# A planned order for attention and a gated MLP on one core: each DMA counted with its pieces and a limit of eight, other gates for kept weights, and new offsets

## The chip, the core and the metric

The kernel runs on one core of one Trainium2 chip. The metric is the device time of one execution in microseconds (us). A core has five engines with an instruction queue each: TensorE (PE) for matmuls, VectorE (DVE), ScalarE (ACT), GpSimd (POOL), and SyncE (SP), which here does nothing but issue DMAs. Every engine works its queue in order: an instruction that waits holds up all that stands behind it on that engine.

## The reference

```python
# q, k, v: (8, 8, 576, 64) float32; g_norm: (64,)
# moe_w_in: (512, 2048) float64, moe_w_out: (2048, 512) float64
kv  = np.einsum('bhsd,bhse->bhde', k, v)
out = np.einsum('bhsd,bhde->bhse', q, kv)
rms = np.sqrt(np.mean(out * out, axis=-1, keepdims=True) + 1e-06)
attn = (out / rms * g_norm).astype(np.float32)
x = attn.transpose(0, 2, 1, 3).reshape(4608, 512)
h = x @ w_in                       # 4608 x 2048
g = h * np.cos(h)
result = (g @ w_out).astype(np.float32)   # 4608 x 512
```

Nearly all of the arithmetic is in the two products with w_in and w_out.

## The kernel before, in words

**Tiling.** The 4608 tokens are cut into nine chunks of 512, the 2048 columns of w_in into sixteen pieces of 128, j = 0 to 15. Each operand of a product is split into a high and a low float32r part, and a product is three matmuls (high by high, high by low, low by high). The weights come as float64; their bits are taken apart and joined to float32 on ACT and DVE (`w_part`), then split.

**Stages.** Attention gives the x tiles of a chunk, four per chunk (p = 0 to 3, two heads each): `x_front_part` for chunks 0 and 1, `x_part` for the others. An x tile of the later kind begins with a load of q in four DMAs for each batch that the chunk touches (`q_loads`: eight where it touches two), then a transpose on DVE (`qT`). Chunks 0 to 2 are worked by 48 *steps* (chunk, j): `stage1_part` makes h for 128 columns in a PSUM bank, `act_part` makes g = h cos h on ACT and DVE (ki, r, then the split into ghi and glo), and `stage2_part` multiplies it into the accumulators acc. The order of the steps is chunk 0 with j 0 to 3, chunk 1 with j 0 to 7, then the remainders of both, then chunk 2; partial results of the first two segments go to DRAM and come back later (`part`). One step is 24 matmuls of 512 columns.

**Pairs.** Chunks 3 to 8 are worked two at a time. There the first product is done with seven products in place of eight (`quad_part`): the four quarters A11 to A22 of the operands and sums and differences of them, S1 to S4. `cross_part` makes these of the x tiles, `sums_part` makes them of w_in, once, piece pair m = 0 to 7 at a time. The split weights don't stay in SBUF: during the steps they are stored in DRAM, w_in's quarters and w_out by `keep_in` and `keep_out`, w_in's sums by `sums_part`; the arrays are `wq` and `wod`. From the first pair on they are loaded back as they are needed (`load_in`, `load_out`), and the space of the weights holds the operands of the pairs. The x tiles of chunks 3 and 4 are stored in DRAM too when they are ready (`x<-slot` in the profile) and come back when there is room for them (`wo<-x`, `xhi<-x`, `xlo<-x`).

**The order.** All of this is written as generators that yield requests: run on an engine for a modelled time with a priority (an earlier due time goes first), wait for events, take a buffer. `Order.run` is a small planner that runs while the kernel is built: it takes the request that can start first, by its own model of when engines are busy, and in that order the instructions are emitted and pinned. So the modelled costs decide the place of every instruction on its engine, and nothing of the model is in the kernel itself. On the chip an instruction starts as soon as its operands are there and its engine has come to it, so a DMA can be issued long before or after its planned time. The model has half speed for PE in the beginning and behind gaps (`slow`), and one access path that POOL and DVE share for some operations (`POOL*`, `DVE*`). The table `haste` holds an offset in us to the due time for each piece of work, found by a search outside the kernel; `put_off` reads it, and `step_off` reads offsets of gates, a quarter of the value in whole steps. A gate is an event that fires when the first product of a step, or a product of a pair, is planned, and lets other work begin.

**DMA in the model before.** `load` and the other senders request "SP" for the issue time of all their DMAs together (`issue_us`), emit them, then request "DMA" for a data time (`us`), one after the other, and the data count as landed `DMA_LAT` = 1.9 us later. In the trace SP at times waits for an earlier DMA to land before it issues the next one; the model before has no such limit.

All instructions go through a helper class, so that the profile puts nearly every one at line 225; groups are told apart by the names of their tiles.

Of the kernel before, what the change touches and what calls it, by code (L numbers as in the profile page):

```python
# [49 lines left out]
class Order:  # L50
# [84 lines left out]
    def run(self):  # L135
        while self.pending:
# [18 lines left out]
            proc = item[4]  # L155
# [16 lines left out]
def tile_kernel(  # L172
# [129 lines left out]
    KEEP, SUMS = 16, 18  # L302
# [3 lines left out]
    def due(i):  # L306
# [7 lines left out]
        ('acc', 0): -5.4, ('acc', 1): 203.3, ('acc', 10): 61.1, ('acc', 11): -32.4, ('acc', 12): -0.2,  # L314
        ('acc', 13): 113.7, ('acc', 14): 49.1, ('acc', 15): 149.6, ('acc', 16): -14.2, ('acc', 17): -14.6,
        ('acc', 19): -52.9, ('acc', 2): 50.3, ('acc', 20): 60.1, ('acc', 21): 215.4, ('acc', 22): -12.9,
        ('acc', 23): 75.5, ('acc', 24): 241.3, ('acc', 25): -23.3, ('acc', 26): -47.0, ('acc', 27): -6.6,
        ('acc', 29): 28.5, ('acc', 30): -51.1, ('acc', 31): 111.0, ('acc', 32): 20.4, ('acc', 33): 133.8,
        ('acc', 34): -195.5, ('acc', 35): 47.6, ('acc', 36): 59.4, ('acc', 37): 7.2, ('acc', 38): -35.1,
        ('acc', 39): -9.7, ('acc', 4): 124.9, ('acc', 40): -86.2, ('acc', 41): 247.6, ('acc', 42): 70.7,  # L320
        ('acc', 43): 6.6, ('acc', 44): 11.9, ('acc', 46): -38.4, ('acc', 47): 9.9, ('acc', 5): -14.3,
        ('acc', 6): 49.4, ('acc', 7): -37.8, ('acc', 8): 18.3, ('acc', 9): -0.2, ('act', 0): -46.6,
        ('act', 1): -60.5, ('act', 10): 39.5, ('act', 11): 33.6, ('act', 12): -13.8, ('act', 13): -156.4,
        ('act', 14): 13.0, ('act', 15): -102.7, ('act', 16): 17.7, ('act', 17): 24.0, ('act', 18): -19.1,
        ('act', 19): -12.1, ('act', 2): -180.3, ('act', 20): 9.6, ('act', 21): 49.5, ('act', 22): 2.2,
        ('act', 23): -118.6, ('act', 24): 5.8, ('act', 25): 59.1, ('act', 26): -1.5, ('act', 27): 229.0,
        ('act', 28): -66.9, ('act', 29): -40.3, ('act', 3): -10.9, ('act', 30): -95.6, ('act', 31): -40.1,
        ('act', 32): 2.5, ('act', 33): 2.9, ('act', 34): -17.2, ('act', 36): -21.4, ('act', 37): -50.0,
        ('act', 38): -51.6, ('act', 4): -0.4, ('act', 40): 14.6, ('act', 41): -7.3, ('act', 42): 28.4,
        ('act', 43): 112.9, ('act', 44): 0.7, ('act', 45): 176.9, ('act', 46): -31.5, ('act', 47): -36.8,  # L330
        ('act', 6): 2.1, ('act', 7): -3.0, ('act', 8): 20.7, ('act', 9): 22.9, ('combine by', 0, 0, 1): -15.7,
# [1352 lines left out]
```

## Time and profile before

| what | value |
|---|---|
| median of 3 runs (lowest, highest) | 848.12 us (846.54, 849.31) |
| profiled execution: its own time | 848.17 us |
| its span, first to last instruction | 846.4 us |
| PE busy, share of the span | 826.7 us, 98% |
| DVE, ACT, POOL busy | 602.0, 501.3, 236.0 us |
| mean granted clock of PE | 0.989 |
| DMA bytes, mean rate | 181.22 MB, 214 GB/s |

The span is what the views of the profile cover; the execution's own time holds 1.8 us more. Busy time is the time in which an engine had at least one instruction under way. Idle time of PE and a granted clock below 1 are what PE loses; an idle stretch of another engine counts only where PE ends up waiting for it. The DMA rows tell issues and the median time from issue to landing; a row of SPq in the order of time is SP's time at the issue itself, with any wait inside it.

### The profile page before, as it was taken

The numbers are of one execution on the slowest core, as the hardware profiler recorded it, in microseconds if no ns is written. First come the engines' busy times: TensorE is split into PE (matmuls) and PEld (weight loads), VectorE is DVE, ScalarE is ACT, GpSimd is POOL, SyncE is SP. The second block draws the span as 40 slices with busy tenths as digits, with TensorE's granted clock in tenths as the row PEclk, the third lists the DMA queues.
The fourth block names the chain that finished last, engine by engine and source line by source line (L and its number), as shares of the span: only waits on it lengthen the run. The fifth ranks groups of instructions, "written<-read, shape, count | busy, mean of one in ns | idle before, by whom it ended". The sixth has DMA issues, their size and how long they took to land.

```text
span 846.4 us, 12697 instructions
## 1 busy us (share of the span) xinstructions
PE 826.7 (98%) x4376; PEld 683.9 (81%) x4376; DVE 602.0 (71%) x953; ACT 501.3 (59%) x984; POOL 236.0 (28%) x151
## 2 busy tenths in 40 slices
PE   6999999999989998999999999999999999999998
PEld 6778888888877886888888888888888888888886
DVE  4898899748767888888899789788686621466111
ACT  3888786436445465686777657767566523465321
POOL 2410000223225463213332771452242011101211
PEclk7999999999999999999999999999999999999999
DMA  9997006896485597888678657876557657663663
GB/s 308 321 367 250 12 0 236 268 300 185 148 265 172 136 279 218 263 256 267 218 214 305 209 195 191 245 226 203 193 174 250 190 188 244 193 196 108 230 207 135
DMA packets 150913, 181.22 MB, mean 214 GB/s; under 512 B 74432, under 2 KB 114112, under 8 KB 150848
## 3 DMA queue, kind: packets, MB, share of 16 engines
q1 hardware_dynamic: 150336, 179.68, 67.7%
q8 instruction: 35, 0.57, 0.3%
q10 hardware_dynamic: 512, 0.72, 0.2%
q14 instruction: 30, 0.25, 0.1%
HBM read 143.66 MB, written 36.70 MB: 213 GB/s over the span
## 4 chain that ended last, share of the span: by engine, by line
PE 59%; DMA 3%; DVE 1%; ACT 1%; SPq 1%; POOL 0%; issue 0%; DVEq 0%
PE acc L225 31%; PE bank L225 28%; DMA sg<-in_v_dram 1%; SPq L225 1%; DMA x<-slot 1%; ACT wi L225 0%; POOL rinv L225 0%; DVE slot L225 0%; DMA qb<-in_q_dram 0%; DMA wo<-x 0%; DVE xlo L225 0%; DVE sg L225 0%; DVE wi L225 0%; ACT ghi L225 0%; DVE r L225 0%
## 5 line engine op out<-in xcount | busy, mean ns | idle before, releaser
L225 PE MATMUL acc<-wo,ghi 128*128 128x512 f32 x1152 | 356.4, 390 | 0.0
L225 PEld LDWEIGHTS acc<-wo,ghi 128*128 128x128 f32 x1152 | 214.9, 188 | 44.1
L225 PE MATMUL bank<-wi,wo 128*128 128x512 f32 (+2 forms) x1092 | 245.0, 379 | 4.5 <-ACT wi L225 2.9
L225 PEld LDWEIGHTS bank<-wi,wo 128*128 128x128 f32 (+2 forms) x1092 | 192.2, 185 | 46.5 <-ACT wi L225 4.1
L225 PE MATMUL acc<-wo,glo 128*128 128x512 f32 x576 | 224.3, 389 | 0.0
L225 POOL TENSOR_TENSOR rinv<-ms,mhalf 128x16 f32<-128x16 f32 (+1 forms) x36 | 99.2, 2759 | 149.4 <-DVE ms L225 143.4
L225 PEld LDWEIGHTS acc<-wo,glo 128*128 128x128 f32 x576 | 108.1, 188 | 22.7
L225 PE MATMUL bank<-xhi,wi 128*128 128x512 f32 x320 | 100.7, 396 | 3.3 <-DVE r L225 3.3
L225 POOL TENSOR_TENSOR glo<-wo,ghi 128x512 fp32r<-128x512 f32 x28 | 38.1, 1359 | 175.1 <-ACT ghi L225 175.1
L225 ACT CAST ghi<-wo 128x512 fp32r<-128x512 f32 x69 | 42.8, 621 | 61.6 <-PE acc L225 60.6
L225 PEld LDWEIGHTS bank<-xhi,wi 128*128 128x128 f32 x320 | 60.1, 190 | 16.4 <-DVE r L225 4.4
L225 DVE TENSOR_TENSOR wi<-bank,wi 128x512 f32<-128x512 f32 x72 | 49.7, 690 | 32.5 <-PE bank L225 27.7
L225 ACT ACTIVATE ki<-bank 128x512 int32<-128x512 f32 x72 | 42.8, 594 | 43.0 <-PE bank L225 36.1
L225 DVE TENSOR_TENSOR glo<-wo,ghi 128x512 fp32r<-128x512 f32 x41 | 28.8, 703 | 55.1 <-ACT ghi L225 52.8
L225 PE MATMUL bank<-xlo,wi 128*128 128x512 f32 x160 | 63.1, 394 | 0.0
L225 ACT CAST ghi<-r 128x512 fp32r<-128x512 f32 x60 | 37.1, 618 | 37.0 <-PE acc L225 34.0
L225 ACT ACTIVATE ki<-wi 128x512 int32<-128x512 f32 x72 | 45.1, 627 | 22.7 <-DVE wi L225 17.2
L225 ACT COPY wi<-bank 128x512 f32<-128x512 f32 x72 | 42.0, 585 | 27.4 <-PE bank L225 25.6
L225 ACT ACTIVATE wo<-wo 128x512 f32<-128x512 f32 x69 | 43.4, 630 | 21.6 <-DVE wo L225 21.2
L225 DVE TENSOR_TENSOR glo<-r,ghi 128x512 fp32r<-128x512 f32 x54 | 39.3, 727 | 20.1 <-ACT ghi L225 17.8
L225 DVE SCALAR_TENSOR_TENSOR r<-bank,ki 128x512 f32<-128x512 f32 x51 | 34.9, 683 | 15.1 <-ACT ki L225 14.8
L225 ACT ACTIVATE r<-r 128x512 f32<-128x512 f32 x60 | 37.6, 628 | 11.0 <-DVE r L225 10.8
(178 smaller groups left out, 1079.6 us busy)
## 6 DMA issues: line engine op xcount, KB each, us to landing
wo<-wod SPq DMA_DIRECT2D x96, 512.0 KB, 3.4
wo<-wq SPq DMA_DIRECT2D x84, 512.0 KB, 4.1
out_dram<-slot SPq DMA_DIRECT2D x35, 256.0 KB, 3.3
wo<-in_moe_w_out_dram SPq DMA_DIRECT2D x16, 512.0 KB, 8.8
wi<-in_moe_w_in_dram SPq DMA_DIRECT2D x16, 512.0 KB, 9.5
wod<-wo SPq DMA_DIRECT2D x16, 512.0 KB, 3.9
wq<-wi SPq DMA_DIRECT2D x24, 256.0 KB, 3.0
m<-in_k_dram SPq DMA_DIRECT2D x24, 256.0 KB, 5.1
```

What stands on the lines that cost most here:

```text
L225: return lambda *a, **kw: tc.keep_in_program_order(f(*a, **kw))
```

## The change

Four things are changed, all in how the order is planned, but for the second.

1. The planner counts DMAs one by one. A sender tells the number of its DMAs, their issue time (0.48 us each unless told otherwise) and the data time of all of them. Each DMA is issued when SP is free and the eighth before it has landed; its data follow those before it, and it has landed 1.9 us behind its data. Several data times are other numbers than before; the q loads of chunk 1, which are issued once for two head pairs, are counted once for two; the first k and v loads, which ACT issues, take next to no time of SP.
2. Of the two tiles of sums of w_in, the one for S1 and A22 is stored in two DMAs in place of four.
3. Kept weights: the first gate is step 6 in place of 16, and each piece can have an offset of its gate.
4. The table of offsets is a new one throughout (11 of 720 keys in either table have the same value in both).

```diff
+    ISSUE, LANDING = 0.48, 1.9
...
+        self.landed, self.sent = [0.0] * 8, 0
...
     def begin(self, e, t):
+        if e == "DMA":
+            return t
...
             end = start + d
+            if e == "SP":
+
+                n, us = options[0][2:]
+                end, data = start, self.busy["DMA"]
+                for _ in range(n):
+                    end = max(end, self.landed[self.sent % 8]) + d / n
+                    data = max(data, end) + us / n
+                    self.landed[self.sent % 8] = data + self.LANDING
+                    self.sent += 1
+                self.busy["DMA"] = proc.data = data
+            if e == "DMA":
+                proc.t = proc.data + self.LAT
+                self.advance(proc, (e, proc.data + self.LAT))
+                continue
...
-    KEEP, SUMS = 16, 18
+    KEEP, SUMS = 6, 18
...
-    DMA_LAT = 1.9
+    DMA_LAT = sched.LANDING
 
-    def load(issue_us, us, prio, event, issue, wait=(), take=None):
+    def send(n, us, issue=sched.ISSUE):
+
+        return "SP", issue * n, n, us
+
+    def load(sends, prio, event, issue, wait=(), take=None):
...
-            yield "run", [("SP", issue_us)], prio
+            yield "run", [sends], prio
             issue(*slot)
-            _, end = yield "run", [("DMA", us)], -1e3
+            _, end = yield "run", [("DMA", 0.0)], -1e3
...
-            yield "run", [("SP", 1.9)], prio
-            for half, q in enumerate(places):
-                for n, part in enumerate((hi.bitcast(F32), t)):
+            yield "run", [send(2 if places[0] < places[1] else 4, 1.5)], prio
+            for n, part in enumerate((hi.bitcast(F32), t)):
+                if places[0] < places[1]:
+                    sync.dma_start(
+                        out=wq[:, 7 * m + S1:7 * m + A22 + 1:A22 - S1, n], in_=part.rearrange("p (a f) -> p a f", a=2))
+                    continue
+                for half, q in enumerate(places):
                     sync.dma_start(out=wq[:, 7 * m + q, n], in_=part[:, half * WH:(half + 1) * WH])
-            _, end = yield "run", [("DMA", 0.8)], -1e3
+            _, end = yield "run", [("DMA", 0.0)], -1e3
...
-            load(0.9, 2.4 if c else 2.1, t, [kv_in[c, p]] + ([] if c or p else [g_in]), kv_loads_front(c, p, lend(2, [kv_used[c, p]])))
+            load(send(2, 2.4 if c else 2.1, sched.ISSUE if c or p else 0.05), t, [kv_in[c, p]] + ([] if c or p else [g_in]), kv_loads_front(c, p, lend(2, [kv_used[c, p]])))
...
-            load(0.9 if c else 0.45, 1.1 if c else 0.75, t, [q_in[c, p]], q_loads_front(c, p, key))
+            if c == 0:
+                load(send(1, 0.75), t, [q_in[c, p]], q_loads_front(c, p, key))
+            elif p % 2 == 0:
+                load(send(3, 2.2), t, [q_in[c, p], q_in[c, p + 1]], q_loads_front(c, p, key))
...
-        load(0.48, 1.4 if key[0] == "wi" else 1.33, t, [w_in[key]], w_loads(key), wait=lent.get(key, ()))
+        load(send(1, 1.45 if key[0] == "wi" else 1.35), t, [w_in[key]], w_loads(key), wait=lent.get(key, ()))
...
-        load(1.3, 0.4, due(i) - 6.0, [over_in[b,]], over_loads(b), wait=[begun] + ([kv_used[b - 1, NP - 1]] if b > FRONT else []))
+        load(send(2, 1.85, 0.63), due(i) - 6.0, [over_in[b,]], over_loads(b), wait=[begun] + ([kv_used[b - 1, NP - 1]] if b > FRONT else []))
...
-            load(1.95 * len(chunk_parts(c)), 1.6, due(i) - 6.0, [q_in[c, p]], q_loads(c, p), wait=[gates[max(i - LEAD, 0)]], take=t_q)
+            load(send(4 * len(chunk_parts(c)), 1.8), due(i) - 6.0, [q_in[c, p]], q_loads(c, p), wait=[gates[max(i - LEAD, 0)]], take=t_q)
...
         i = KEEP + j * (NS - KEEP - 8) // NJ
+        i = min(max(i + step_off("gate keep", j), 0), NS - 4)
         sched.spawn(gated(i, keep_in(j, due(i + 6))))
         sched.spawn(gated(i, keep_out(j, due(i + 6) + 1.0)))
```

Of the new offsets (us) the prediction speaks of these, with those before in brackets: loads of w_in pieces 0, 1, 2: -93.4, -156.3, -565.4 (-713.3, -109.2, -10.3); load of k and v of chunk 1's second head pair: -293.9 (-129.7); sums 4 and 6: 566.9 and 1219.0 (1421.5 and 79.3); gates of kept pieces 1, 2, 4, 6, 10, 13, 14, 15: -38.4, -6.0, -12.6, -0.3, 3.5, -28.6, 14.3, -10.5 (none).

The other senders (kept weights and their loads, results, the x tiles that are set aside) get `send` in the same way: one DMA of 256 KB counts 0.75 us of data as before, a load of 512 KB of kept weights 1.52 in place of 1.4.

More of the change, by code (lines that the diff above doesn't have):

```diff
@@ L319, in tile_kernel @@
[L319 to L323, printed above, removed]
@@ new lines, in tile_kernel @@
+        ('split', 76): -42.9, ('split', 77): 56.0, ('split', 78): 70.5, ('split', 8): -3.8, ('split', 80): 0.6,
+        ('split', 81): -38.8, ('split', 82): -32.9, ('split', 83): -71.2, ('split', 84): -123.8,
+        ('split', 85): -7.4, ('split', 86): 51.3, ('split', 87): 239.6, ('split', 88): -4.2, ('split', 89): -16.2,
+        ('split', 9): 1.1, ('split', 90): -34.0, ('split', 91): 11.2, ('split', 93): 0.6, ('split', 94): 104.5,
+        ('split', 95): 127.6, ('sums by', 0): -125.8, ('sums by', 1): -152.1, ('sums by', 2): -17.5,
@@ L466, in tile_kernel @@
+        ('gate keep', 10): 3.5, ('gate keep', 14): 14.3, ('gate x', 5, 2): 1.7, ('gate keep', 4): -12.6,
     }
@@ L975, in x_norm @@
         if c in ASIDE:
-            yield "run", [("SP", 0.4)], prio
+            yield "run", [send(1, 0.75)], prio
             aside = tc.dram_tile([P, CH], F32, name=f"x{c}_{p}")
             sync.dma_start(out=aside, in_=x)
-            _, end = yield "run", [("DMA", 0.75)], -1e3
+            _, end = yield "run", [("DMA", 0.0)], -1e3
             sched.give(t_slot, end + DMA_LAT, held)
@@ L984, in x_norm @@
             yield "wait", [stored]
-            yield "run", [("SP", 0.37)], due(begin[PLAIN - 1]) + p
+            yield "run", [send(1, 0.75)], due(begin[PLAIN - 1]) + p
             x = store_tile(held)
             sync.dma_start(out=x, in_=aside)
-            _, end = yield "run", [("DMA", 0.75)], -1e3
+            _, end = yield "run", [("DMA", 0.0)], -1e3
             end += DMA_LAT
@@ L1185, in out_part @@
         if before is not None:
-            yield "run", [("SP", 0.42)], prio
+            yield "run", [send(1, 0.75)], prio
             sync.dma_start(out=o, in_=before)
-            _, end = yield "run", [("DMA", 0.75)], -1e3
+            _, end = yield "run", [("DMA", 0.0)], -1e3
             come = Event()
@@ L1200, in out_part @@
         sched.give(t_acc[t], end)
-        yield "run", [("SP", 0.4)], prio
+        yield "run", [send(1, 0.75)], prio
         if complete:
@@ L1206, in out_part @@
             sync.dma_start(out=partial[c, t], in_=o)
-        _, end = yield "run", [("DMA", 0.75)], -1e3
+        _, end = yield "run", [("DMA", 0.0)], -1e3
         sched.give(t_slot, end + DMA_LAT, slot)
@@ L1250, in keep_in @@
         yield "wait", [w_done["wi", j]]
-        yield "run", [("SP", 0.5 * (2 - j % 2))], prio
+        yield "run", [send(2 - j % 2, 0.75 * (2 - j % 2))], prio
         w, m = w_split["wi", j], j // 2
@@ L1255, in keep_in @@
                 out=wq[:, 7 * m + q], in_=w[:, :, half * WH:(half + 1) * WH].bitcast(F32))
-        _, end = yield "run", [("DMA", 0.75 * (2 - j % 2))], -1e3
+        _, end = yield "run", [("DMA", 0.0)], -1e3
         sched.fire(wi_kept[j], end + DMA_LAT)
@@ L1260, in keep_out @@
         yield "wait", [w_done["wo", j]]
-        yield "run", [("SP", 0.4)], prio
+        yield "run", [send(1, 1.3)], prio
         sync.dma_start(out=wod[j], in_=w_split["wo", j].bitcast(F32))
-        _, end = yield "run", [("DMA", 1.4)], -1e3
+        _, end = yield "run", [("DMA", 0.0)], -1e3
         sched.fire(wo_kept[j], end + DMA_LAT)
@@ L1338, in load_in @@
             slot = yield "take", t_win
-            yield "run", [("SP", 0.37)], due(NS + 2 * t * QUAD // 7) - 14.0
+            yield "run", [send(1, 1.52)], due(NS + 2 * t * QUAD // 7) - 14.0
             w = wpool.tile([P, 2, 2, WH], F32R, name=f"wo{slot}")
@@ L1342, in load_in @@
             sync.dma_start(out=w.bitcast(F32), in_=wq[:, s:s + 2])
-            _, end = yield "run", [("DMA", 1.4)], -1e3
+            _, end = yield "run", [("DMA", 0.0)], -1e3
             win_tiles[t] = w, slot
@@ L1351, in load_out @@
             slot = yield "take", t_wout
-            yield "run", [("SP", 0.37)], due_unit(u) - 12.0
+            yield "run", [send(1, 1.52)], due_unit(u) - 12.0
             w = wpool.tile([P, 2, DM], F32R, name=f"wo{slot}")
             sync.dma_start(out=w.bitcast(F32), in_=wod[j])
-            _, end = yield "run", [("DMA", 1.4)], -1e3
+            _, end = yield "run", [("DMA", 0.0)], -1e3
             wout_tiles[u] = w, slot
```

136 lines of the change are left out of this document (66 added, 70 removed), and 156 rows, old and new, of the table haste.

## The prediction

> **What bounds the kernel now.** First the page's summary, then TensorE (PE) in stretches of 20 us (columns: stretch, length, busy us and instructions of PE, PEld, DVE, ACT, POOL, then granted clock, DMA share, GB/s).
>
> ```profile
> span 846.4 us, 12697 instructions
> PE 826.7 (98%) x4376; PEld 683.9 (81%) x4376; DVE 602.0 (71%) x953; ACT 501.3 (59%) x984; POOL 236.0 (28%) x151
> ...
> 0.00:20.00 20.00, 13.65 (x152) 12.38 (x154) 7.88 (x17) 7.74 (x15) 6.07 (x14) 0.78 0.96 310
> 20.00:40.00 20.00, 18.57 (x223) 15.40 (x220) 16.57 (x33) 16.24 (x40) 7.08 (x5) 0.96 1.09 315
> 80.00:100.00 20.00, 20.00 (x90) 16.57 (x89) 16.50 (x29) 14.77 (x28) 0.00 (x0) 1.00 0.18 32
> 100.00:120.00 20.00, 20.00 (x90) 16.53 (x90) 18.66 (x32) 17.50 (x33) 0.00 (x0) 1.00 0.00 0
> 240.00:260.00 20.00, 17.86 (x77) 14.48 (x76) 14.35 (x25) 11.62 (x26) 6.18 (x2) 0.91 0.76 241
> 260.00:280.00 20.00, 18.12 (x151) 14.85 (x150) 15.96 (x29) 9.34 (x24) 11.28 (x6) 1.00 0.49 152
> 320.00:340.00 20.00, 17.27 (x93) 13.60 (x89) 17.15 (x21) 11.50 (x23) 8.37 (x7) 0.91 0.76 217
> 340.00:640.00 300.00, 299.37 (x1469) 247.68 (x1468) 253.34 (x388) 211.54 (x420) 119.71 (x67) 1.00 0.73 226
> 640.00:840.00 200.00, 200.00 (x884) 165.58 (x884) 80.06 (x119) 81.89 (x141) 24.49 (x19) 1.00 0.60 194
> ```
>
> PE is the bound: idle for 846.4 - 826.7 = 19.7 us. The opening holds 6.35 + 1.43 of these, three stretches between 240 and 340 hold 2.14 + 1.88 + 2.73 = 6.75, the 500 us from 340 to 840 only 0.63; most of the rest is the tail behind the last matmul. Two stretches also show a clock of 0.91: 20 x 0.09 = 1.8 us lost in each. So a new order can win 6.75 + 3.6 = 10.35 us between 240 and 340, something in the opening, and next to nothing elsewhere; the matmuls themselves stay.
>
> Next, PE in order of time at these places (start, us, instructions, and in brackets the idle time before it), and what its releasers waited for.
>
> ```profile
> 248.96 0.72 PE L225 MATMUL bank<-xhi,wi 128*128 128x512 f32 x2 [2.14 <-DVE r L225]
> 269.31 0.73 PE L225 MATMUL bank<-xhi,wi 128*128 128x512 f32 x2 [1.19 <-DVE r L225]
> 334.25 0.73 PE L225 MATMUL bank<-wi,wo 128*128 128x512 f32 x2 [2.30 <-ACT wi L225]
> 335.41 4.83 PE L225 MATMUL bank<-wi,wo 128*128 128x512 f32 x13 [0.42 <-DVE wi L225]
> ```
>
> ```profile
> 247.62 0.71 DVE L225 STREAM_TRANSPOSE qT<-qb 128x512 f32<-128x512 f32 x1 [2.14 <-DMA qb<-in_q_dram]
> ...
> 265.41 0.62 ACT L225 CAST wi<-xhi 128x512 fp32r<-128x512 f32 x1 [5.04 <-DMA xhi<-x]
> ...
> 331.18 1.76 DVE L225 TENSOR_TENSOR xlo<-xhi,slot 128x512 f32<-128x512 f32 x1
> 334.07 0.68 DVE L225 TENSOR_TENSOR slot<-slot,xhi 128x512 f32<-128x512 f32 x1
> ```
>
> First stall: the in-order DVE sat 2.14 us on the transpose of a q tile whose load had not landed; the multiply that frees the next product's bank stood behind it. Second: ACT sat 5.04 us on a reloaded x tile, with a ki behind it. Third: PE passes from chunk 2 to the first chunk pair, whose split operands come late. All three begin as late DMAs. Now SP's queue, which issues them, and the chain of waits before the third.
>
> ```profile
> 236.17 5.32 SPq L225 DMA_DIRECT2D qb<-in_q_dram  x8
> 242.09 3.85 SPq L225 DMA_DIRECT2D qb<-in_q_dram  x8
> 256.87 0.99 SPq L225 DMA_DIRECT2D wq<-wi  x2
> 260.49 0.81 SPq L225 DMA_DIRECT2D xhi<-x  x1
> ```
>
> ```profile
> 313.29 6.09 DMA x<-slot
> ```
>
> Eight q pieces take 3.85 us to issue when nothing holds SP and 5.32 us behind other loads; kept-weight stores stand right ahead of the reload of 260.49; a store of 256 KB took 6.09 us to land.
>
> **The change, part by part.**
>
> *The planner's DMA model.* It issues no instruction; it decides where each pinned DMA and its consumers stand. Before, a q load of eight pieces is 3.9 us of SP plus 1.6 of data, whatever is under way, so the 1.47 us by which the issue at 236.17 exceeds 3.85 is unplanned, and so is part of the 6.09 (the old plan allows 0.75 + 1.9). The new one gives each DMA its issue time, holds SP at eight outstanding, and raises data times: the leftover k/v rows from 0.4 to 1.85 us in six loads (+8.7), the stores of sums from 0.8 to 1.5 in sixteen (+11.2). That is about 20 us of DMA time which the old order did not see, and by the gates in the code all but the last two leftover loads (2.9 us) come before the pairs begin, where the stalls are. An order made with these costs puts the transposes, casts and reloads later in DVE's and ACT's order, behind work that is ready. I take the first stall as gone with its clock loss, 2.14 + 1.8 = 3.94.
>
> Would the clock loss go along? A pair of products right behind the 2.14 us gap, and the one that starts 0.87 us later:
>
> ```profile
> 249.75 0.63 PE L225 MATMUL bank<-xhi,wi 128*128 128x512 f32 x2
> 250.62 1.05 PE L225 MATMUL bank<-xhi,wi 128*128 128x512 f32 x2
> ```
>
> The same pair takes 0.63 and then 1.05, and the stretch shows 0.91, while the 1.19 us gap left its stretch at 1.00. So a gap of some 2 us costs 1.8 more, and with the gap the loss goes. The Trainium skill (TensorE: Matmul & The Clock Gate, Part 1, the table of the two states) has the half clock come only after an idle window of about 3.4 us. By that rule neither gap would have cost clock, and the gain below would be 2.7 us smaller, 844.5 us; the trace disagrees (0.91 after 2.14 us idle) and decides, so this gets no chance of its own.
>
> *Kept weights from step 6 on.* Sixteen pairs of stores (256 or 512 KB of w_in, 512 KB of w_out) get earlier gates: the last five were gates 32 to 38, and are now 29, 31, 26, 38, 35; the first five were 16 to 22, and are now 6, 0, 9, 12, 11 (integer parts of the formula and of the new offsets divided by 4). A step is 24 matmuls of 0.227 us (3 in the 0.68 us of the chain of waits), 5.4 us, so three of the last five move up by 16 to 49 us, away from 250, where they stand now. They fall where DMA is idle (share 0.18 and 0.00 from 80 to 120) and cost nothing there. Their cover early is the weight loads' lead (the first product, and the w_out loads issued in the first 66 us):
>
> ```profile
> 34.73 0.71 PE L225 MATMUL bank<-xhi,wi 128*128 128x512 f32 x2
> ...
> wo<-in_moe_w_out_dram SPq DMA_DIRECT2D x15, 512.0 KB, 9.2
> ```
>
> By 66 us 15 of the 16 pieces of w_out are requested, and PE, which begins its products at 34.73, is in its sixth step of 48. Without that cover a pair of 1 MB would delay a weight by 2.8 us, at the 372 GB/s of 35 to 66:
>
> ```profile
> 20.00:34.70 14.70, 13.27 (x198) 11.00 (x194) 11.80 (x24) 12.59 (x34) 6.38 (x4) 0.95 1.10 291
> 34.70:66.00 31.30, 30.98 (x217) 24.53 (x216) 28.96 (x52) 25.19 (x50) 6.48 (x4) 1.00 1.07 372
> ```
>
> With three pairs out of the way of the reload I take the second stall (1.19) as gone, and leave the rest of that stretch's 1.88, for which no DMA is named.
>
> *Sums in fewer DMAs.* 48 instead of 64: one tile of each pair goes out in two DMAs of 256 KB, the other still in four of 128 KB. No row shows the new shape; the nearest are
>
> ```profile
> wq<-wi SPq DMA_DIRECT2D x24, 256.0 KB, 3.0
> wq<-slot SPq DMA_DIRECT2D x32, 128.0 KB, 3.0
> wo<-x SPq DMA_DIRECT2D x4, 256.0 KB, 3.8
> qb<-in_q_dram SPq DMA_DIRECT2D x32, 40.0 KB, 2.3
> ```
>
> A 256 KB store in the same 1 KB runs lands as soon as a 128 KB one, so a tile comes free between 0.8 us earlier and 0.8 later (3.0 against 3.8): I take 0, since nothing reads a sum before the first pair's weights are loaded. SP saves 16 issues of about 0.45 (3.85 / 8 is 0.48): 7 us, hidden in its waits, worth something only through the first two stalls, already counted.
>
> *The third stall.* Its cause is mixed: the 6.09 us landing, but also DVE at 1.76 us for an operation that takes 0.68 three lines later, while POOL works on a sum of w_in, which shares the way to memory in the planner's own costs (begin):
>
> ```profile
> 330.79 1.61 POOL L225 TENSOR_TENSOR m<-sg,m 128x512 f32<-128x512 f32 x1
> ```
>
> The old planner knows of that contention already. Bounds: nothing gained, or 2.73 + 1.8 = 4.53. I take half, 2.27.
>
> *The new search.* All 700 or so offsets change, so the order is new everywhere. Opening: w_in piece 2 and chunk 1's second head pair now load before chunk 0 is complete, w_in piece 0 drops from sixth to about fifteenth. From 20 to 34.7 DVE is busy 11.80 and ACT 12.59 of 14.7: elementwise work, not the loads, sets the first product. One more or one less weight split ahead of it is four DVE operations:
>
> ```profile
> L225 DVE SCALAR_TENSOR_TENSOR sg<-sg,m 128x512 int32<-128x512 int32 x12 | 8.2, 685 | 1.9 <-ACT sg L225 1.7
> L225 DVE SCALAR_TENSOR_TENSOR sg<-wi,sg 128x512 int32<-128x512 int32 x6 | 4.1, 683 | 0.0
> L225 DVE TENSOR_TENSOR wi<-sg,wi 128x512 fp32r<-128x512 f32 x6 | 4.1, 683 | 0.0
> L225 DVE TENSOR_SCALAR m<-wi 128x512 int32<-128x512 uint32 x4 | 1.7, 418 | 0.0
> ```
>
> 0.685 + 0.683 + 0.683 + 0.418 = 2.5 us. I take 0, with -2.5 and +2.5 as ends. From 66 on a new order makes small stalls of its own; 340 to 640 has 0.63 us in 300, and I allow 1.0 in all. The tail stays.
>
> Sum: -3.94 - 1.19 - 2.27 + 1.0 = -6.4. The profiled execution took 848.17 us (its span and 1.8 around it; the median of the runs is 848.12): 848.17 - 6.4 = **841.8 us**.
>
> **The rivals.**
>
> *The stalls only move.* For it: the eight-piece loads stay, most gates of the q loads are the same numbers as before, and one late landing in front of an in-order DVE is enough. Against: the model now counts what was late. One new stall of the first kind costs 3.94, two 7.9: 841.8 + 7.9 = 849.7, no difference to be told. A measurement of this kernel can't tell less than 0.3%, 2.5 us, from no change.
>
> *Slower: the handover from chunk 2 to the first pair grows.* Sums 4 and 6 have offsets of +567 and +1219, which put them behind all other work of their engines; POOL then does them around 320 to 335, and a DVE operation that meets one costs 1.76 - 0.68 = 1.08 more. Eight more like the row above make the operands 8.6 us late with nothing else for PE to do, and the third stall's 2.27 isn't won: 841.8 + 2.3 + 8.6 = 852.7. It decides once that stall has grown by 6.6 us, since the other places win 4.1. Against: sum 4 stood at +1421 before, and the planner prices the contention.
>
> *More than forecast.* All 10.35 go and the opening wins a split: 848.17 - 10.35 - 2.5 = 835.3. For it: 340 to 840 shows that such orders can run with hardly a gap. Against: the third stall's second cause, and an opening bound by elementwise work.
>
> *The change doesn't do what it says*: the limit is of the planner's counting, and where landings differ (a q piece of 40 KB 2.3 us, a store 3.0, a reload 3.8, against a constant 1.9 behind the data) the order is no better founded than before. Its time is that of the moved stalls.
>
> **How the numbers follow.** Forecast 0.57; stalls moved (with the change without effect) 0.20; handover slower 0.15; more than forecast 0.08. Faster than 845.6: nearly all of the forecast, the 0.08, and a little of the moved stalls, 0.65. Slower than 850.7: the handover and some of the moved stalls, 0.18. Between: 0.17. The forecast's own range is 839 (third stall wholly gone) to 845.7 (one new stall); for 8 in 10 it reaches down to 836.5 and up to 851, halfway into both outer cases.
>
> **What would show it.** Right: no gap over 2 us on PE between 66 and 340 and a clock of 1.00 in all of these stretches, no DVE transpose or ACT cast with over 1 us of wait for qb or a reloaded x in front of a bank's release; kept-weight stores between 80 and 120; 48 stores of sums. Wrong: a first product later than 37, a gap over 4 us where the pairs begin, or gaps between 340 and 640 adding up to more than 2.

## The result, and the profile after

| | before | after |
|---|---|---|
| median, four runs of each beside each other (lowest, highest) | 847.33 us (846.44, 849.31) | 840.12 us (839.29, 841.59) |
| ratio, 95% interval | | 0.9914 [0.9889, 0.9938] |
| profiled execution | 848.17 us | 839.29 us |
| its span | 846.4 us | 837.5 us |
| mean granted clock of PE | 0.989 | 0.995 |

The kernel is faster by 7.2 us, 0.86%; the forecast was 6.4. The two profiled executions lie 8.9 apart, the one of after being the fastest of its four, and the accounts below are made between these two.

The page of the changed kernel, its summary:

```profile
PE 822.7 (98%) x4376; PEld 681.5 (81%) x4376; DVE 597.2 (71%) x959; ACT 503.5 (60%) x982; POOL 229.0 (27%) x147
```

The changed kernel in stretches, with the columns of the prediction's first table (after POOL come the granted clock, the DMA share and GB/s):

```profile
0.00:66.00 66.00, 56.14 (x554) 46.73 (x555) 47.32 (x90) 45.32 (x97) 18.95 (x21) 0.95 1.00 334
...
80.00:100.00 20.00, 20.00 (x90) 16.54 (x89) 17.34 (x29) 16.01 (x30) 0.00 (x0) 1.00 0.51 178
...
240.00:260.00 20.00, 20.00 (x94) 16.78 (x94) 16.39 (x29) 10.69 (x27) 9.94 (x4) 1.00 0.64 191
260.00:280.00 20.00, 20.00 (x161) 16.68 (x160) 17.23 (x31) 10.71 (x23) 9.43 (x6) 1.00 0.41 137
320.00:340.00 20.00, 19.02 (x84) 15.12 (x83) 17.35 (x28) 14.23 (x25) 5.52 (x4) 1.00 0.91 290
66.00:340.00 274.00, 273.02 (x1503) 226.78 (x1502) 225.11 (x381) 168.45 (x333) 62.20 (x36) 1.00 0.64 198
340.00:640.00 300.00, 299.70 (x1468) 247.80 (x1467) 241.74 (x369) 206.48 (x410) 127.22 (x75) 1.00 0.73 225
```

Between 240 and 280 PE no longer stops, at full clock; of the third stall 0.98 us is left. From 66 to 340 PE is idle for 0.98 us where it was 6.75, and from 340 to 640 for 0.30 where it was 0.63. The share of DMA from 80 to 100 is up from 0.18 to 0.51, since kept weights are stored there.

PE of the changed kernel in order of time (the first product, the one gap behind 66 us, the last matmul):

```profile
37.34 0.70 PE L243 MATMUL bank<-xhi,wi 128*128 128x512 f32 x2
...
339.21 0.96 PE L243 MATMUL bank<-wi,wo 128*128 128x512 f32 x3 [0.98 <-ACT wi L243]
...
833.46 0.39 PE L243 MATMUL acc<-wo,glo 128*128 128x512 f32 x1
```

Two q transposes and a reloaded x tile on DVE of the changed kernel, and the cast of the other reloaded x tile on ACT; no brackets mean no wait:

```profile
243.16 0.70 DVE L243 STREAM_TRANSPOSE qT<-qb 128x512 f32<-128x512 f32 x1
...
251.53 0.71 DVE L243 STREAM_TRANSPOSE qT<-qb 128x512 f32<-128x512 f32 x1
...
318.64 0.69 DVE L243 TENSOR_TENSOR slot<-wo,wo 128x512 f32<-128x512 f32 x1 [1.70 <-DMA wo<-x]
...
259.16 0.62 ACT L243 CAST wi<-xhi 128x512 fp32r<-128x512 f32 x1 [0.88 <-DMA xhi<-x]
```

SP's queue of the changed kernel at the place of the first two stalls:

```profile
222.00 0.62 SPq L243 DMA_DIRECT2D k_over<-in_k_dram  x1
222.67 0.85 SPq L243 DMA_DIRECT2D v_over<-in_v_dram  x1
...
232.26 3.79 SPq L243 DMA_DIRECT2D qb<-in_q_dram  x8
...
236.64 3.87 SPq L243 DMA_DIRECT2D qb<-in_q_dram  x8
...
245.25 4.30 SPq L243 DMA_DIRECT2D qb<-in_q_dram  x8
...
252.26 3.83 SPq L243 DMA_DIRECT2D qb<-in_q_dram  x8
...
256.14 0.45 SPq L243 DMA_DIRECT2D xhi<-x  x1
```

Two rows of SP's queue of before, shortly ahead of its load of 236.17:

```profile
233.51 0.62 SPq L225 DMA_DIRECT2D k_over<-in_k_dram  x1
234.18 0.71 SPq L225 DMA_DIRECT2D v_over<-in_v_dram  x1
```

The pieces of a q tile still take 3.8 to 4.3 us to issue. What changed is when the loads go out. Before, DVE stood at its transpose from 245.48 on (2.14 us ahead of 247.62), when the issue of 242.09, which loads that tile, still had 0.46 to go. Ahead of that load SP had issued the leftover rows of k and v (233.51), and the q load of 236.17, for a tile of chunk 4 that DVE transposes only at 284.74. In the changed kernel the same leftover rows go out at 222.00 and the load for chunk 4 at 232.26. So the load that DVE needs next goes out at 236.64, 5.45 us earlier than before, and DVE transposes 2.65 us after the end of that issue (243.16 - 240.51) without a wait. DVE itself comes 2.32 us earlier than before, not later. The reload of x, too, goes out earlier, at 256.14 in place of 260.49, behind a q load and not behind a row of weight stores; ACT waits 0.88 us for it in place of 5.04.

The sums' stores of the changed kernel, among the DMA issues (count, KB each, median us to landing): 48, as the prediction says.

```profile
wq<-slot SPq DMA_DIRECT2D x8, 256.0 KB, 4.0
wq<-m SPq DMA_DIRECT2D x8, 256.0 KB, 4.1
wq<-slot SPq DMA_DIRECT2D x16, 128.0 KB, 3.9
wq<-sg SPq DMA_DIRECT2D x16, 128.0 KB, 3.6
```

### The profile page after: what moved, and what is told of

Read it like the earlier page. It is cut to its first block, busy times and chain, and to the rows that moved or that the text cites. A ratio compares the mean times of both kernels' runs of the same rounds, so it can differ in the third digit from the quotient of the medians.

```text
span 837.5 us, 12687 instructions
## 1 busy us (share of the span) xinstructions
PE 822.7 (98%) x4376; PEld 681.5 (81%) x4376; DVE 597.2 (71%) x959; ACT 503.5 (60%) x982; POOL 229.0 (27%) x147
## 4 chain that ended last, share of the span: by engine, by line
PE 92%; DVE 3%; DMA 2%; POOL 1%; ACT 1%; SPq 1%; issue 0%; ACTq 0%; POOLq 0%; DVEq 0%
PE acc L243 46%; PE bank L243 45%; DVE wo L243 1%; POOL rinv L243 1%; DMA wi<-in_q_dram 1%; DMA wo<-wq 1%; SPq L243 1%; DVE wi L243 0%; DVE sg L243 0%; DVE r L243 0%; DVE xhi L243 0%; ACT wo L243 0%; DVE ms L243 0%; POOL m L243 0%; ACT slot L243 0%
## 5 line engine op out<-in xcount | busy, mean ns | idle before, releaser
L243 PE MATMUL bank<-wi,wo 128*128 128x512 f32 (+2 forms) x1092 | 242.1, 378 | 1.3 <-ACT wi L243 1.0
L243 DVE TENSOR_TENSOR glo<-wo,ghi 128x512 fp32r<-128x512 f32 x45 | 34.5, 766 | 39.8 <-ACT ghi L243 39.8
L243 POOL TENSOR_TENSOR glo<-wo,ghi 128x512 fp32r<-128x512 f32 x24 | 32.0, 1332 | 112.3 <-ACT ghi L243 88.2
L243 DVE TENSOR_TENSOR glo<-r,ghi 128x512 fp32r<-128x512 f32 x54 | 37.1, 687 | 10.6 <-ACT ghi L243 10.3
```

Of the source, the lines that this page charges most:

```text
L243: return lambda *a, **kw: tc.keep_in_program_order(f(*a, **kw))
```

## The experiments

The theory on test: PE's stalls between 240 and 340 are late DMAs in front of in-order engines, and the new order takes them away because its plan counts those DMAs. Rivals: another cause (above all for the third stall, contention of DVE and POOL), or a change that won through one of its parts (fewer stores, earlier stores, merely another search) and not by the plan. The runs were made in three groups, each beside runs of the kernel before on the same chip, and each ratio is to these, whose median was 847.92 us for the first (stores early, q in half as many DMAs, and the two experiments on the sums' stores), 848.06 for the second (the changed kernel with q relieved, the old model searched again, and the two mixtures of old and new), 848.78 for the rest. Between groups the ratios are compared.

### The order of before, with its DMAs relieved

**Kept weights stored early.** Nothing moves but the stores of kept pieces 11 to 15, which are issued where the piece is ready; the planner still counts them at the old place.

```
         w_split[key] = w
+        if key[1] >= 11:
+            if key[0] == "wi":
+                store_in(key[1], w, key[1] // 2)
+            else:
+                sync.dma_start(out=wod[key[1]], in_=w.bitcast(F32))
...
-        for q, half in ((A11, 0), (A12, 1)) if j % 2 == 0 else ((S4, 1),):
+        if j < 11:
+            store_in(j, w, m)
```

> The kernel before with its order as it is, but the stores of kept weights for the last five pieces of w_in and w_out (j 11 to 15, which stand at 247 to 260 us) are emitted where the split of the piece ends, some 100 us earlier. Theory that crowded DMAs make the stalls, and that kept stores in front of the reload made the second: the wait of ACT for xhi<-x (5.04) shrinks to below 3, PE's gap at 269 (1.19) goes, the first gap at 249 (2.14, its q load stands ahead of these stores) stays within 0.5; time -1 to -2.5 us of the kernel before. Rival, that the gates of the kept weights are what the change lives on: two or three of the gaps go, -5 us or more. Rival, that they play no part: the 1.19 stays, 0.

Measured: 847.06 us, ratio 0.9985 [0.9963, 1.0008]. PE, DVE and SP of this run:

```profile
250.66 1.22 PE L225 MATMUL bank<-xhi,wi 128*128 128x512 f32 x2 [3.58 <-DVE r L225]
...
256.24 0.34 SPq L225 DMA_DIRECT2D xhi<-x  x1
...
333.86 0.73 PE L225 MATMUL bank<-wi,wo 128*128 128x512 f32 x2 [2.60 <-ACT wi L225]
...
249.32 0.71 DVE L225 STREAM_TRANSPOSE qT<-qb 128x512 f32<-128x512 f32 x1 [3.57 <-DMA qb<-in_q_dram]
...
322.00 0.69 DVE L225 TENSOR_TENSOR slot<-wo,wo 128x512 f32<-128x512 f32 x1 [3.13 <-DMA wo<-x]
```

The gap at 269 is gone: from 260 to 280 PE is busy for all of the 20 us. The reload of x goes out at 256.24 in place of 260.49, and ACT does not wait for it any more. So the kept-weight stores were the cause of that gap. But the first gap grew from 2.14 to 3.58, where at most 0.5 more was expected, and no gain can be told: moving these stores alone did not win the 1.88 us of their stall.

**q in half as many DMAs.** A q tile is loaded by one DMA for each batch and head, in long runs. The tokens then lie in other places, so it isn't the reference's result; sizes, engines and order stay. The edit changes two things at once: SP issues half as many DMAs, and the pieces that the DMA engines move are longer (150,913 packets in all before, 98,560 with the edit, for the same 181.2 MB). Which of the two counts for more is not separated here.

```
-                    for f in range(2):
-                        e = 2 * j + f
-                        sync.dma_start(
-                            out=qb[32 * e:32 * e + 32, o0 // 32:(o0 + n) // 32, :],
-                            in_=q[b, 2 * p + j, s0:s0 + n, 32 * f:32 * f + 32].rearrange("(tb t) d -> t tb d", t=32),
-                        )
+                    sync.dma_start(
+                        out=qb[64 * j:64 * j + 64, o0 // 32:(o0 + n) // 32, :],
+                        in_=q[b, 2 * p + j, s0:s0 + n, :].rearrange("s d -> (s d)").rearrange("(r a c) -> r a c", r=64, c=32),
+                    )
```

> The kernel before with its order as it is, but each q load of x_part takes half as many DMAs, in long runs (four where there were eight); the tokens then lie in other places of the tile, so the output is not the reference's, and all later work is the same in size. Theory that late q pieces make the first stall: the issue of a two-batch load falls from 3.85 to some 1.9 us, DVE's wait for qb at 247 (2.14) and PE's gap at 249 go, and the clock of 240 to 260 is 1.00; time -4 us or, with something at the other two stalls, down to -8. Rival, that the order of DVE and ACT alone makes the gap: it stays above 1.5, within -1 us of the kernel before.

Measured: 839.86 us, ratio 0.9909 [0.9881, 0.9936], 8.1 us gained. PE and ACT of this run in order of time, then the stretch of the third stall:

```profile
248.67 0.72 PE L225 MATMUL bank<-xhi,wi 128*128 128x512 f32 x2 [0.92 <-DVE r L225]
...
267.94 0.74 PE L225 MATMUL bank<-xhi,wi 128*128 128x512 f32 x2 [1.75 <-DVE r L225]
...
264.04 0.62 ACT L225 CAST wi<-xhi 128x512 fp32r<-128x512 f32 x1 [5.68 <-DMA xhi<-x]
```

```profile
320.00:340.00 20.00, 19.90 (x88) 16.13 (x87) 19.65 (x26) 13.40 (x26) 7.47 (x7) 1.00 0.78 251
```

With the order of before, q in half as many DMAs gives as much as the whole change gives. The first stall falls to 0.92 and keeps its clock; the second stays, as it must if kept-weight stores make it. The third is all but gone, 0.10 us idle in its stretch, though no operation of DVE or POOL was touched.

**Both.** The two edits together.

> The order of the kernel before with both reliefs, q in half as many DMAs with long runs (tokens in other places, output not the reference's) and the stores of kept pieces 11 to 15 emitted at their split. Alone the first left gaps of 0.92, 1.75 and 0.37 on PE between 240 and 340, the second removed the gap at 269. Theory that late DMAs are the whole loss there: at most 1 us of gaps is left, time 836.5 to 839. Rival, that a part of the gaps is the order of DVE and ACT itself: over 2 us stay, time 839.5 to 842.

Measured: 837.73 us, ratio 0.9869 [0.9851, 0.9888]. The stretch from 66 to 345:

```profile
66.00:345.00 279.00, 278.26 (x1527) 231.18 (x1526) 231.10 (x375) 171.71 (x343) 76.89 (x48) 1.00 0.61 199
```

PE is idle for 0.74 us in 279, at full clock. In the order of before, then, late DMAs are the whole loss between 240 and 340 but for at most these 0.74 us. The early stores, for which no gain could be told alone, go with a further 2.1 us by the medians (839.86 to 837.73, of two groups of runs) and 3.4 by the ratios (0.9909 to 0.9869, whose intervals overlap a little), once q is relieved.

### The sums' stores

**Two DMAs in the order of before.** Only the stores of the tile for S1 and A22 become two; the plan knows nothing of it.

```
+                if places[0] < places[1]:
+                    sync.dma_start(
+                        out=wq[:, 7 * m + S1:7 * m + A22 + 1:A22 - S1, n], in_=part.rearrange("p (a f) -> p a f", a=2))
+                    continue
```

> The kernel before with its order as it is, but the S1 and A22 tile of sums stored in two DMAs in place of four, as in the changed kernel; the planner counts them as before. By the prediction's term this saves SP 16 issues, some 7 us in its waits, and is worth 0 by itself: within 1 us. Rival, that fewer DMAs under the limit of eight bring the q loads forward: -2 us or more, with the first or third gap shorter.

Measured: 843.82 us, ratio 0.9958 [0.994, 0.9977], 4.1 us gained. PE and DVE of this run in order of time:

```profile
249.84 1.17 PE L225 MATMUL bank<-xhi,wi 128*128 128x512 f32 x2 [3.01 <-DVE r L225]
...
333.13 0.73 PE L225 MATMUL bank<-wi,wo 128*128 128x512 f32 x2 [1.13 <-ACT wi L225]
334.29 4.84 PE L225 MATMUL bank<-wi,wo 128*128 128x512 f32 x13 [0.42 <-DVE wi L225]
...
248.50 0.71 DVE L225 STREAM_TRANSPOSE qT<-qb 128x512 f32<-128x512 f32 x1 [3.00 <-DMA qb<-in_q_dram]
...
321.25 0.69 DVE L225 TENSOR_TENSOR slot<-wo,wo 128x512 f32<-128x512 f32 x1 [1.65 <-DMA wo<-x]
```

The prediction's zero for this edit is refuted. The second and third stalls shrink (PE is idle for 1.12 us from 260 to 280 in place of 1.88, and the third gap is 1.13 in place of 2.30), the first grows in this execution. Its profile shows only 1.8 us less span than that of before (844.6 against 846.4), less than the medians do; where the rest lies it doesn't show.

**Four DMAs again in the changed kernel.** The plan stays that of the changed kernel.

```
-            for n, part in enumerate((hi.bitcast(F32), t)):
-                if places[0] < places[1]:
...
+            for half, q in enumerate(places):
+                for n, part in enumerate((hi.bitcast(F32), t)):
                     sync.dma_start(out=wq[:, 7 * m + q, n], in_=part[:, half * WH:(half + 1) * WH])
```

> The changed kernel with its order as it is, but all sums stored in four DMAs again (64 in place of 48); the planner counts two for half of them. By the prediction's term 0: within 1 us of the changed kernel, 839 to 842. Rival: the freed issue time carries part of the gain, and this kernel is 2 us or more slower than the changed one, with a new gap on PE between 140 and 340.

Measured: 841.03 us, ratio 0.993 [0.9905, 0.9955], against 0.9914 of the changed kernel. PE in order of time has two small gaps that the changed kernel has not:

```profile
306.58 0.72 PE L243 MATMUL bank<-xhi,wi 128*128 128x512 f32 x2 [0.67 <-DVE r L243]
...
326.54 0.50 PE L243 MATMUL acc<-wo,glo 128*128 128x512 f32 x1 [0.85 <-DVE glo L243]
```

By the ratios the two are 1.4 us apart, with intervals that overlap, so no difference is shown. The same relief was worth 4 us in the old order, where DMAs are late.

### The changed kernel, with q relieved

The same edit of the q loads in the changed kernel.

> The changed kernel with its order as it is and q loaded in half as many DMAs with long runs, as in before_q_long (tokens in other places of the tile, so the output is not the reference's; all work the same in size). That edit won some 8 us on the order before. Theory that the new order already gives the q pieces the time that they take: hardly anything is left to win, 0 to -1.5 us of the changed kernel's 840.1, so 838.5 to 840.5. Rival, that the gain of the change came from elsewhere and q pieces are still late: -3 us or more.

Measured: 840.8 us, ratio 0.9923 [0.9897, 0.9949], nothing gained. The same gap remains on PE:

```profile
339.47 5.75 PE L243 MATMUL bank<-wi,wo 128*128 128x512 f32 x24 [1.02 <-ACT wi L243]
```

The edit that gave 8.1 us on the old order gives none on the new one. So the new order has already removed the loss that the edit removes.

### The model against the search

The table of offsets belongs to the model it was searched for: the new table under the old model, or the reverse, makes no complete order. So each kernel here has a table of its own, found by a random search over the offsets for an early planned end. Each edit is a new table beside what the heading says.

**The old model, searched again.**

```
     haste = {
-        ('acc', 0): -5.4, ('acc', 1): 203.3, ('acc', 10): 61.1, ('acc', 11): -32.4, ('acc', 12): -0.2,
...
```

> The code of the kernel before with another table of offsets, searched afresh on its own planner until it planned PE's last matmul at 830.7 us. The kernel before planned 824.9 and its profile shows 842.2, 17.3 later; the changed kernel planned 826.9 and shows 833.8, 6.9 later; the execution's time is some 6 us more than PE's end. Theory that the old DMA model is what misleads: about 17 us late again, PE ends near 848 and the time is 850 to 858, with DVE and ACT waiting for q pieces or reloads. Rival, that the kernel before had an unlucky order and any new search would do: some 7 us late, time 842 to 846.

Measured: 862.85 us, ratio 1.0184 [1.0156, 1.0211], slower still than the 850 to 858 expected. PE in order of time, two of its gaps:

```profile
271.38 1.22 PE L225 MATMUL bank<-xhi,wi 128*128 128x512 f32 x2 [3.00 <-DVE r L225]
...
407.10 2.90 PE L225 MATMUL bank<-wi,wo 128*128 128x512 f32 x6 [3.19 <-DMA wo<-wq]
```

**The same with q in half as many DMAs.**

> The second order made on the old model, as it is, with q loaded in half as many DMAs with long runs (tokens in other places of the tile, so the output is not the reference's). Theory that orders of the old model suffer from DMAs that it counts too low, q pieces first: 6 to 15 us less than its 862.9, with no DVE wait over 1 us for q pieces. Rival, that its lateness has nothing to do with DMA: within 3 us.

Measured: 843.49 us, ratio 0.9945 [0.9924, 0.9966]. It is 19.4 us faster than the same order with all q pieces (20 by the ratios, as the two are of different groups), more than expected. Of PE's waits for weights at 397 and 407 one of 0.86 us is left. DVE still waits 1.83 us for a q tile (transpose at 245.84), where no wait over 1 was expected. A second order of the old model thus also loses its time to DMAs that come later than its plan has them.

**The new model, searched again.** The code of the changed kernel, with another table, from a search that began at a shuffled one.

> The changed kernel's code with another table of offsets, searched afresh on the new DMA model from a shuffled start; it plans PE's last matmul at 834.5. The orders made on the old model ended 17.3, 29.6 and 12.6 us behind their plans, the changed kernel 6.9, the one with the new model and late kept weights 9.9. Theory that the new model with early kept weights keeps its plans: 6 to 9 us late, PE ends at 840.5 to 843.5, time 846 to 849.5. Rival, that the changed kernel's order was a lucky one: over 12 us late, time 852 or more.

Measured: 848.63 us, ratio 1.0 [0.9986, 1.0015]. PE in order of time, its largest gap behind 240:

```profile
258.94 1.10 PE L243 MATMUL bank<-xhi,wi 128*128 128x512 f32 x2 [1.75 <-DVE r L243]
```

A table made for the new model is not enough: this one is no faster than the kernel before. Its plan ends 7.6 us later than that of the changed kernel, and the chip adds 2.7 more. DVE waits 3.0 us for q and ACT 5.4 for a reloaded x here too. But two of PE's three gaps of over 1 us are in the plan itself: when this kernel is built, its planner leaves PE idle for 2.66 and 1.11 us in front of the same products where the profile shows 2.08 and 1.08. The third is 1.75 in the profile; the plan has one of 1.40, four products later. So the model foresaw most of these gaps, and the search had not found a table without them. In the plan of before only the first of the three stalls shows, with 0.94 us.

**The old model with gates from step 6 and two DMAs for the sums.** The second and third parts of the change without the first.

```
-    KEEP, SUMS = 16, 18
+    KEEP, SUMS = 6, 18
```

> The planner's old DMA model with the changed kernel's gates for kept weights (first gate 6, own offsets) and its two-DMA sums, offsets searched afresh; it plans PE's last matmul at 837.0. Theory that the model is what counts: some 17 us late, time 856 to 864. Rival, that the earlier kept weights and fewer sums carry the gain: some 7 us late, time 847 to 852.

Measured: 853.53 us, ratio 1.006 [1.0038, 1.0083]. Its plan ends at 837.0, worse than that of before, and holds a planned stall of 8.17 us; PE's last matmul ends 12.6 us after the plan, between what the two theories expected.

**The new model with gates from step 16 and four DMAs for the sums.** The first part without the second and third.

> The planner's new DMA model with the gates of kept weights as before (first gate 16, no offsets) and all sums in four DMAs, offsets searched afresh; it plans PE's last matmul at 832.7. Theory that the model is what counts: some 7 us late, time 843 to 848, no wait of DVE or ACT for q pieces over 1 us. Rival, that kept weights and sums carry it: some 17 us late, 853 to 859.

Measured: 848.9 us, ratio 1.0016 [1.0003, 1.0029], above the 843 to 848 expected. PE, ACT and SP of this run:

```profile
252.13 0.72 PE L243 MATMUL bank<-m,kv_w 128*128 128x192 f32 x2 [5.25 <-DVE r L243]
...
249.53 0.62 ACT L243 CAST wi<-xhi 128x512 fp32r<-128x512 f32 x1 [5.48 <-DMA xhi<-x]
...
245.21 1.22 SPq L243 DMA_DIRECT2D xhi<-x  x1
```

DVE waits for no q tile between 240 and 340, but the second stall is there, larger: the reload of x is issued at 245.21, behind stores of kept weights, and lands 4.3 us later. The plan has 1.02 us of this gap.

**The same with the stores of kept pieces 11 to 15 early**, by the edit of the first experiment.

> The kernel with the new model and late kept weights, its order as it is, but the stores of pieces 11 to 15 emitted where their split ends. There ACT waited 5.48 us for the reload of a set-aside x tile, whose load stands behind such stores, and PE 5.25 us behind that. Theory that the earlier gates of kept weights are the part of the change that saves the reload: that gap falls below 2 us, time 4 to 7 us less than the 848.9 of the kernel with late stores. Rival, that the reload is late by itself: the gap stays above 4, within 1 us.

Measured: 851.36 us, ratio 1.0029 [1.001, 1.0048], against 1.0016 without the edit, where a gain was expected. PE in order of time:

```profile
168.31 0.69 PE L243 MATMUL bank<-sg,m 128*64 128x64 f32 x16 [1.76 <-DMA sg<-in_v_dram]
...
254.55 0.54 PE L243 MATMUL bank<-m,kv_w 128*128 128x192 f32 x2 [2.75 <-DVE r L243]
```

The gap falls from 5.25 to 2.75, so the stores are about half of its cause. A new stall appears at 168, where PE waits for loads of v; some of the moved stores stand ahead of these on SP. That they cause it is likely, not shown.

For the four orders searched anew with all q pieces, and for before and after, the kernel's own planner gives an end for PE's last matmul when it is built; the profile gives the real one:

| order | planned, us | measured, us | late by |
|---|---|---|---|
| old model: before | 824.9 | 842.2 | 17.3 |
| old model: searched again | 830.7 | 860.3 | 29.6 |
| old model: gates from 6, sums in two | 837.0 | 849.6 | 12.6 |
| new model: after | 826.9 | 833.85 | 6.9 |
| new model: searched again | 834.5 | 844.1 | 9.6 |
| new model: gates from 16, sums in four | 832.7 | 842.65 | 9.9 |

The second order's profile is of its slowest execution, 3.3 us above its median, so its 29.6 is some 3 us too high. The plan of after ends 2.0 us later than that of before, and the chip ends it 8.3 earlier. In every order of the new model the chip stays within 10 us of the plan, in every one of the old model it is over 12 us late. With q relieved, the two old orders end at 836.05 and 838.03, 11.1 and 7.3 after the same plans, and with both reliefs the order of before ends at 832.14, 7.2 after its plan. So what a plan of the old model misses is mostly DMAs, and the new model misses less of it.

That a kernel gets faster by the new model alone is not shown. Of its three tables here one gains 7 us, and the other two are as slow as the kernel before, since their plans end 6 to 8 us later. The changed kernel needed both a plan that the chip keeps and a table with a short plan; how long each table was searched is not on record, and three against three are few. How the gain splits between the limit of eight, the data times and the earlier gates was not separated, since none could be changed without a new table, and tables differ by as much.

## Why the prediction was right, and where it was not

It was right in its sign, in its size (841.8 against 840.1) and in the cause of the loss: the stalls begin as late DMAs in front of in-order engines, and the new order is without the first two. In two points it was lucky. It took from the code that an order made with the new costs would avoid these stalls, but the same code with another table takes 848.63 us; this table is a good one. And two steps of its working, how the first stall goes and half of the third stall's cause, were wrong without harm to the sum. Four rows of before are needed for the terms, and one of the run with q in half as many DMAs. DVE at the third stall, the last matmul, and the reload in the chain of waits:

```profile
322.38 0.69 DVE L225 TENSOR_TENSOR slot<-wo,wo 128x512 f32<-128x512 f32 x1 [2.83 <-DMA wo<-x]
...
841.78 0.39 PE L225 MATMUL acc<-wo,glo 128*128 128x512 f32 x1
...
319.40 2.89 DMA wo<-x
```

the slow DVE operation of the third stall in the run with q in half as many DMAs:

```profile
326.57 1.77 DVE L225 TENSOR_TENSOR xlo<-xhi,slot 128x512 f32<-128x512 f32 x1
```

and the first 66 us of before as one stretch:

```profile
0.00:66.00 66.00, 57.89 (x558) 47.91 (x559) 48.63 (x91) 45.51 (x97) 18.92 (x21) 0.92 1.04 335
```

| term of the sum | predicted, us | measured between the two profiles, us |
|---|---|---|
| first stall and its clock | -3.94 | -3.94 |
| second stall | -1.19 | -1.88 |
| third stall and its clock | -2.27 | -3.55 (4.53 less the 0.98 left) |
| small stalls elsewhere | +1.0 | -0.33 (0.63 to 0.30) |
| tail behind the last matmul | 0 | -0.6 (4.2 to 3.65) |
| opening | 0 | +1.4 (what is left of the 8.9) |
| sum | -6.4 | -8.9 |

**First stall.** It went as predicted, the clock loss with it. That the lateness is of q pieces is shown: with q in half as many DMAs the gap of the old order falls to 0.92. The step on how it goes was wrong. The prediction has the new order put the transpose later on DVE, behind work that is ready. In both traces it stands ten DVE instructions behind the q transpose before it (235.97 and 235.13), and DVE comes to it 2.32 us earlier than before. What moved is the load, which goes out 5.45 us earlier, with the leftover k and v rows 11.5 us earlier out of its way. These rows are the loads whose counted data time rose from 0.4 to 1.85; whether that or the new offsets moved them is not shown.

**Second stall.** The cause was right (early stores remove it in the old order); the rest of 0.69, for which the profile named no DMA, went with it.

**Third stall.** Here the step failed that called its cause mixed and took half. DVE's wait for the reloaded x and PE's gap go together over four runs of the old order: 2.83 and 2.30 in before, 3.13 and 2.60 with the kept weights early, 1.65 and 1.13 with fewer stores, no wait and no gap with fewer q pieces; the gap is the wait less 0.52 or 0.53. The slow DVE operation beside POOL's sum, the other half of the prediction's cause, is in the last of these runs as it was, 1.77 us at 326.57, without a gap. So it costs PE next to nothing there. The 6.09 us landing that the prediction quoted is the head of the chain: the x tile stored at 313.29 has landed at 319.38, its reload goes out at 319.40 and takes 2.89 us, and DVE, which has waited 2.83 us, starts at 322.38. Put at its full 4.53, the term would have been 1 us too high, as 0.98 of the gap is left.

**Sums in fewer DMAs.** The step "I take 0" failed by 4 us for the old order. It looked at when a tile comes free and held 7 us of SP's time hidden by its waits. The likely reason is that SP's time is not free where the loads that stalls wait for stand in the same queue: DVE's wait for the reloaded x fell from 2.83 to 1.65. Since those stalls go with the new order anyway, the sum suffered little; in the new order no gain of the edit is shown. On the landing, 4.0 us for the new 256 KB stores in the changed kernel is above the bounds of 3.0 and 3.8, but the 128 KB ones beside them take 3.9 and 3.6, so the size makes little difference, as the prediction says.

**Kept weights.** "Where DMA is idle" was right in kind (the share from 80 to 100 is now 0.51), and PE loses nothing there. The count was off: of the last five pieces four get an earlier gate (32, 34, 35 and 38 become 29, 31, 26 and 35), not three, and one a later one (37 becomes 38). Their own worth is not settled: no gain alone in the old order, 2.1 to 3.4 us together with the relief of q, and no gain in the new model's order with late gates (ratios 1.0016 and 1.0029).

**Opening.** Predicted 0 within 2.5: PE is idle for 9.86 of its 66 us where it was 8.11, at a higher clock, and the first product is 2.6 us later, at 37.34, past the 37 that the prediction set as a sign of being wrong. What the other terms leave of the 8.9 puts its cost at 1.4, inside the bounds; it was not measured by itself.

**The new search.** No fresh stalls of a us came up, so the allowance of 1.0 was too much for this table. As a rule it would be too little: the other table of the same model has gaps of 2.08, 1.75 and 1.08, most of which its plan has too. The lower end of the prediction's own range, the third stall wholly gone, is 839.5 by its terms, not 839.

**The rivals.** A handover that grows did not come: POOL idles from 315.34 to 333.58, and the remaining gap is 0.98. Stalls that only move are what happened in three of the experiments (the early stores in both orders, and the new table), so the rival, with its chance of 0.20, was a fair one; with another table of the same code it would have come true.

## What to carry to other kernels

When a planned order is late on the chip, compare the planner's end with the real one first, and look for what its model doesn't count before searching further: here 10 of 17 us of lateness went when q came in half as many DMAs and the stores of the last five kept pieces went out earlier. An issue that is "hidden" on a DMA queue can still delay a load behind it, so price it by the first in-order consumer that waits for that queue. And a better model is half of it: the order it allows must still be found, and its planned end tells whether it was. A relief that is worth 8 us on one order may be worth nothing on another; test it on the order that will be used.

## What was not expected of the hardware

**Half clock.** In before a gap of 2.14 us was followed by half clock, and one of 1.19 was not. The length of one gap does not decide. With the kept weights early and with the sums in two, pairs right behind gaps of 3.58 and 3.01 take 1.22 and 1.17 us, against 0.72 behind the 0.92 us gap. But a gap of 1.75 was followed by a pair of 0.74 in one kernel (267.94 above) and of 1.10 in another (258.94 above), and in one and the same execution, of the old model searched again, a gap of 1.93 by a pair of 1.19 (at 249.85) and one of 1.94 by a pair of 0.69 (at 318.89). In the run with the sums in two, even 1.13 and 0.42 us with 0.73 between them were enough: the stretch from 320 to 340 has a clock of 0.91. The Trainium skill (TensorE: Matmul & The Clock Gate, Part 1) has the clock follow the activity in windows of about 3.4 us that run free of the program. The loss of 1.8 us in a stretch at 0.91 is about half of such a window, an estimate. That the phase decides would agree with 1.75 and 1.93 to 1.94 going both ways; that a whole idle window is needed does not agree with half clock behind gaps of 1.75, 1.93 and 2.14.

**DMAs that an engine's queue hides.** Loading q in half as many DMAs, with longer runs and the same bytes, was worth 8.1 and 19.4 us on two orders in which TensorE is busy 98% and 96% of the time. And the same order has a first stall between 2.14 and 3.58 us in three profiles that differ only in stores issued elsewhere, so a gap of this kind is not a fixed number.
